# A hand-ordered SSD and feed-forward kernel: where two state additions stand, and a new order of steps

## The chip, the cores and the metric

One core of a Trainium2 chip runs the whole kernel in one launch. The metric is the device time of one execution in microseconds; the number given for a kernel is the median of its runs. Five engines take part, each with its own instruction queue that runs strictly in order: TensorE (PE, whose weight loads are shown apart as PEld), VectorE (DVE), ScalarE (ACT), GpSimd (POOL), and SyncE (SP), which only sends transfers here. Engines wait for each other through semaphores.

## What is computed

A state-space scan (Mamba-2 SSD) over 4 batches, 8 heads, 768 positions, head size 32 and state size 16, whose output, read as 3072 tokens of 256 features, goes through an RMS norm and a SwiGLU feed-forward of width 1536. The core of the reference:

```python
for c in range(nc):                       # chunks of 32 positions
    cum = np.cumsum(la, axis=-1)          # la = log of the decays a
    L = np.exp(cum[:, :, :, None] - cum[:, :, None, :]) * causal
    M = np.einsum('bhin,bhjn->bhij', Cc, Bc) * L
    y_intra = np.einsum('bhij,bhjd->bhid', M, xc)
    y_inter = np.einsum('bhin,bhnd->bhid', Cc, state) * np.exp(cum)[:, :, :, None]
    y[:, :, sl] = y_intra + y_inter
    Bx = np.einsum('bhjn,bhjd->bhjnd', Bc, xc) * np.exp(cum[:, :, -1:] - cum)[:, :, :, None, None]
    state = np.exp(np.sum(la, axis=-1))[:, :, None, None] * state + np.sum(Bx, axis=2)
...
rms = np.sqrt(np.mean(x * x, axis=-1, keepdims=True) + 1e-06)
xn = x / rms * rms_g
g = xn @ w_gate
silu = g * (1.0 / (1.0 + np.exp(-g)))
return (silu * (xn @ w_val) @ w_out).astype(np.float32)
```

## The kernel before

The 3072 tokens are worked on as twelve pairs of 256 tokens (for the scan) and six blocks of 512 (for the feed-forward). The kernel is a set of small functions, one for each kind of step, and one long text, `order` (from L1193), that lists 1548 steps by hand. A step reads `block:kind.arguments/slot`: `0:y.2/2` calls the kind `y` of block 0 for pair 2 and takes its PSUM buffers from pair slot 2. The steps are run through in this order, and each appends its instructions to the queues of the engines it uses. So the text alone sets in which order each engine does its work; there is no scheduler. A step that is moved in the text moves on every engine it uses, transfers included.

PSUM has three pair slots of two banks each, and two single banks that small results share (`bank`). Later, slots 0 and 1 are turned into the two buffers for gate and value products (step `switch`).

The kinds that matter here, with their lines:

- `fetch.k` sends a piece of a weight matrix (up to 512 KB) on SP's queue. The weights come as 64-bit floats and are converted on the chip: `pow.k` (ACT, L182, L183, L185), `man.k` (DVE, L192, L195), `wt.k` (DVE, L201). `x.p` and `bc.p` send the inputs x, and B and C, of a pair; `gcol` sends the norm's gains.
- The scan of a pair p: `mask`, `sums`, `exp` make the decays L (PE L426, L440, L447, ACT L455). `turn`, `T`, `Tt` transpose B and C (PE L505, L511). `scale` and `Td` put the decays on B and C. `g.p.q` (L555) and `gg.p` (L562) are the products C Bᵀ on PE. `L` and `L1` multiply them into the decays on DVE (L601, L607). `A.p` are the state additions, the sum of Bx, on PE (`additions`, L627); `S.p` makes the new states from them on DVE (L641 to L651). `y.p` are the outputs: for the first two pairs `first_outputs` (L668 for the state part, L677 for the part within a chunk), for later ones `outputs` (L699).
- Pairs 0 and 1 use chunks of 128 positions, later ones of 64. From pair 2 on, `outputs` writes the additions of the next pair into columns of its own y buffers. For pairs 1 and 2 the additions stand as steps of their own, `0:A.1` and `0:A.2`, which take single banks.
- After y: `sq` (ACT, L740 or L747) squares it, `yt` (DVE, L758, or ACT, L763) takes it with the gains, `r`, `row`, `rowe` and `parts` compute rows of decay sums for later pairs (PE L355, L1076; ACT L1089; DVE L362 to L369), `ms` (PE L773) and `rs` make the norm's factor, `xn` and `tx` the normed input and its differences.
- The feed-forward of block 0 begins as plain products: `early.f.s` on the inputs without norm (L837), `gate.f` (L827), with `norm`, `silu`, `hid` behind them. From there on, and in all later blocks, gate and value products use a form with seven products in place of eight: `P.k.j` (PE, L911), `take` (ACT copy, L917), totals `C` (DVE, L923), `silug`/`silu` (ACT, L932), `hidg`/`hid` (DVE, L936); `cw.j` makes the sums of weights it needs (DVE, L881). The output products go the same way: `O.k.f` (L1001), `Otake`, `Oadd`, and `out`, `quarter` send the results.
- `tok` (PE) and `tokout` (an ACT copy) make the sums of decays for all tokens, in a single bank.

The order of block 0 around the steps in question, before: `A.0 S.0 A.1 S.1 g.0.0 ... y.0 ... y.1 r.1 ... row.0 ... early.0.0 ... gate.2 ... gg.2 L1.2.2 L1.2.3 L.2.0 man.8 gate.3 ... A.2 S.2 ... gate.4 ... gate.5 ... y.2 S.3 ... P.2.3 P.1.3 take.1.3 turn.3 ...`

Of the kernel before, what the change touches and what calls it, by code (L numbers as in the profile page):

```python
# [20 lines left out]
def kernel(  # L21
# [35 lines left out]
    P = 128  # L57
    NB, NH, S, D = x.shape
# [5 lines left out]
    T = NB * S  # L64
# [108 lines left out]
    parts = {}  # L173
# [62 lines left out]
    mid = mids[:, 0]  # L236
# [382 lines left out]
    def additions(p, A_ps=None):  # L619
        s = st[p]  # L620
        if A_ps is None:
            A_ps = [bank("A_ps", (P, 2, 2, D)) for u in range(1 if p < 2 else 2)]
        ps["A", p] = A_ps = A_ps if p >= 2 else 2 * A_ps
        for i, u in chunks_of(p)[2]:
            r = slice(0, P) if p < 2 else halves[u]
            for q in range(NQ):
                nc.tensor.matmul(  # L627
                    out=A_ps[u][32 * q:32 * q + 32, i].rearrange("p t d -> p (t d)"),
                    lhsT=s["Bd"][r, i, 2 * q:2 * q + 2].rearrange("p t n -> p (t n)"),
                    rhs=s["x"][r, i, 2 * q:2 * q + 2].rearrange("p t d -> p (t d)"),  # L630
                    start=(i == 0), stop=True, tile_position=(r.start, 32 * q),
                    skip_group_check=True)
# [25 lines left out]
    def first_outputs(p, y):  # L658
# [27 lines left out]
        inter(1, False)  # L686
        del st[p], Ls[p]
# [260 lines left out]
    two = {}  # L948
# [216 lines left out]
    def of_chunk(n, fn):  # L1165
# [29 lines left out]
        0:never 0:after 0:mid 0:fetch.0 0:upto2 0:mids 0:ident16 0:idle.7 0:fetch.1 0:whole16  # L1195
        0:mask.0.0/0 0:whole 0:hmask 0:tmask 0:part 0:gcol 0:part2 0:sel 0:mask.1.1/2 0:after2 0:aT
        0:kinks 0:la0 0:mask.0.1/1 0:log4.0.4 0:fetch.5 0:r.0 0:eps 0:parts.0 0:log 0:d 0:log4.4.2
        0:dx 0:c*2 0:cx 0:scale.0 0:log4.6.2 0:turn.0.1 0:bc.2 0:T.0.1 0:Tt.0.0.1 0:sums.0.1
        0:Tt.0.1.1 0:exp.0.1 0:turn.0.0 0:Tt.0.1.0 0:T.0.0 0:sums.0.0 0:Tt.0.0.0 0:exp.0.0
        0:turn.1.1 0:T.1.1 0:scale.1 0:Tt.1.0.1 0:fetch.2 0:Tt.1.1.1 0:cc 0:g.0.1/1 0:L.0.1  # L1200
        0:turn.1.0 0:Tt.1.1.0 0:Tt.1.0.0 0:sums.1.1 0:T.1.0 0:exp.1.1 0:A.0 0:S.0 0:A.1 0:S.1
        0:g.0.0/0 0:man.0 0:pow.0 0:L.0.0 0:pow.1 0:wt.0 0:last.1 0:man.5 0:mask.1.0/1 0:middles
        0:Tl.1 0:sums.1.0 0:never16 0:fetch.4 0:exp.1.0 0:g.1.0/2 0:fetch.3 0:x.4 0:L.1.0 0:last.0
        0:Tl.0 0:scale.2 0:fetch.6 0:g.1.1/0 0:fetch.7 0:man.1 0:pow.5 0:L.1.1 0:y.0/1 0:wt.5 0:sq.0
        0:fetch.12 0:row.1 0:pow.3 0:rowout.1 0:yt.0 0:ydone.0 0:rowe.1 0:y.1/2 0:r.1 0:fetch.13
        0:row.0 0:man.2 0:fetch.9 0:wt.1 0:early.0.0/0 0:parts.1 0:man.6 0:mask.3/1 0:sums.3 0:pow.2
        0:wt.2 0:rowe.0 0:dT.2 0:sq.1 0:ms.0 0:yt.1 0:ydone.1 0:early.0.1 0:man.3 0:wt.3 0:mask.2/2
        0:sums.2 0:pow.6 0:fetch.8 0:wt.6 0:man.4 0:x.2 0:exp.3 0:early.1.0/1 0:rs.0 0:norm.0 0:xn.0
        0:pow.4 0:wt.4 0:fetch.10 0:man.7 0:dT.3 0:turn.2 0:early.1.1 0:norm.1 0:rowout.0 0:exp.2
        1:table 0:man.9 0:silu.0 0:hid.0 0:gate.2/0 0:T.2 0:Tt.2.0 0:Tt.2.1 0:Td.2 0:pow.7  # L1210
        0:fetch.14 0:wt.7 0:tx.0 0:gg.2/1 0:L1.2.2 0:L1.2.3 0:L.2.0 0:man.8 0:gate.3/2 0:pow.9
        0:fetch.11 0:silu.2 0:hid.2 0:pow.8 0:wt.9 0:wt.8 0:man.11 0:silu.3 0:hid.3 0:A.2 0:S.2
        0:x.3 0:pow.11 0:gate.4/1 0:silu.4 0:hid.4 0:cw.3 0:bc.3 0:scale.3 0:man.10 0:pow.12
        0:gate.5/0 0:silu.5 0:hid.5 0:pow.10 0:y.2/2 0:S.3 0:yt.2 0:sq.2 0:ydone.2 0:switch.1
        0:P.2.3 0:switch.0 0:P.1.3 0:take.1.3 0:turn.3 0:T.3 0:Tt.3.0 0:Tt.3.1 0:wt.10 0:wt.11
        0:P.1.4 0:P.6.3 0:take.6.3 0:man.12 0:Td.3 0:man.13 0:pow.14 0:gg.3/2 0:L1.3.3 0:L.3.0
        0:L1.3.2 0:bc.4 0:scale.4 0:P.2.4 0:P.7.3 0:bc.5 0:scale.5 0:x.5 0:y.3/2 0:wt.12 0:take.7.3
        0:C.11.3 0:P.5.3 0:silug.11.3 0:pow.13 1:S.0 0:fetch.18 0:P.4.3 1:dT.0 0:C.22.3 0:P.3.3
# [12 lines left out]
        0:sub.9 0:tx.1 1:P.6.1 1:take.1.0 1:Tt.0.0 0:hidg.22.5 0:o.11 1:Tt.1.0 2:bc.1 1:take.6.1
        1:P.7.1 0:cw.0 1:P.6.0 1:C.11.1 1:cw.2 1:P.5.1 1:take.7.1 1:C.22.1 1:P.4.1 1:P.2.0 1:C.11.0
        1:P.3.1 1:C.12.1 0:ex.10 0:ex.8 1:take.6.0 1:P.7.0 0:ex.9 1:bc.1 1:P.5.0 1:silu.22.1
        1:silu.21.1 1:bc.0 1:take.7.0 1:hid.21.1 1:P.1.2 1:hid.22.1 1:C.22.0 1:take.1.2 1:silu.11.0
        1:hid.11.0 1:P.4.0 1:silu.21.0 1:hid.21.0 1:silu.12.1 1:hid.12.1 1:P.2.2 1:C.11.2 1:scale2.1
        1:spread.0 1:two.4 1:silu.11.1 1:hid.11.1 1:Tt.0.1 0:table.1 1:P.6.2 1:take.6.2 1:P.3.0
        1:C.12.0 1:P.1.3 1:silu.11.2 1:hid.11.2 1:silu.22.0 1:hid.22.0 1:P.5.2 1:take.1.3 0:put.0
        0:put.3 1:P.7.2 1:take.7.2 1:C.22.2 0:put.2 1:P.6.3 1:take.6.3 1:P.2.3 1:C.11.3 1:silu.11.3
        1:two.2 1:silu.12.0 1:hid.12.0 1:P.4.2 1:silu.21.2 1:hid.21.2 1:P.7.3 1:take.7.3 1:silu.22.2
        1:hid.22.2 1:P.5.3 1:C.22.3 1:P.3.2 1:C.12.2 0:put.1 1:P.4.3 1:silu.21.3 1:hid.21.3  # L1240
        1:hid.11.3 1:silu.12.2 1:hid.12.2 1:x.0 1:P.1.4 1:take.1.4 1:P.3.3 1:C.12.3 1:Tt.1.1 1:Td.1
        2:dT.1 1:s.1 1:s3.1 1:P.1.5 1:take.1.5 1:Td.0 1:P.6.4 1:take.6.4 1:P.2.5 1:C.11.5 1:P.6.5
        1:take.6.5 1:scale2.0 1:P.2.4 1:C.11.4 1:silu.12.3 1:hid.12.3 1:g 1:L1.3 1:L1.2 1:L
        1:silu.11.4 1:hid.11.4 1:P.7.4 1:take.7.4 1:P.7.5 1:take.7.5 1:P.5.4 1:C.22.4 1:silu.22.3
        1:hid.22.3 2:dT.0 1:P.5.5 1:C.22.5 1:y.0 1:x.1 2:S.0 1:s.3 1:P.3.4 1:C.12.4 1:silu.11.5
        1:hid.11.5 1:P.4.5 1:silu.21.5 1:hid.21.5 1:s.0 1:P.4.4 1:silu.21.4 1:hid.21.4 1:silu.22.4
        1:hid.22.4 1:silu.22.5 1:hid.22.5 1:P.3.5 1:C.12.5 1:silu.12.5 1:hid.12.5 1:silu.12.4
        1:hid.12.4 1:O.2.0 1:O.2.1 1:s.2 1:y.1 2:S.1 1:sq 1:yt 1:s.5 1:O.2.2 1:O.1.0 1:O.1.1 1:O.4.0
        1:O.4.1 1:s.4 1:spread.2 1:sub.2 1:O.1.2 1:O.1.3 1:exps 1:O.1.4 1:O.1.5 1:s3.3 1:O.5.0
        1:O.5.1 1:s2.1 1:O.5.2 1:s2.2 1:s2.0 1:O.5.3 1:s2.3 1:s3.0 1:Otake.1 1:spread.1 1:sub.1  # L1250
        1:s3.2 1:ms 1:rs 1:O.5.4 1:O.5.5 1:s2.5 1:s2.4 1:rb 1:ex.2 2:turn.0 2:T.0 2:Tt.0.1 2:Tt.0.0
        1:O.6.0 1:s4.0 1:O.6.1 1:s4.1 1:O.6.2 1:s4.2 1:O.6.3 1:s4.3 2:turn.1 2:T.1 2:Tt.1.0 1:s3.4
        1:s3.5 1:O.6.4 1:s4.4 1:O.6.5 1:Otake.6 1:s4.5 1:O.4.2 1:O.4.3 1:O.7.0 1:O.7.1 1:O.7.2
        1:O.7.3 1:O.7.4 1:O.7.5 1:O.2.3 1:O.4.4 1:O.4.5 1:sub.0 1:ex.0 1:O.2.4 1:O.2.5 1:Otake.7
# [137 lines left out]
```

## Time and profile before

| | us |
|---|---|
| median of three runs | 403.85 (403.8 to 405.18) |
| the profiled execution | 404.06 |
| its span | 402.1 |
| PE busy in it | 394.8 |
| DVE busy | 297.9 |
| ACT busy | 224.5 |

The span is the time from the first to the last instruction; the rest of the execution's time lies around it. The granted TensorE clock is 0.999 of full. In views of groups, a line reads: line, engine, operation, output and input tiles, partitions by elements, count, then busy time and mean. In rows of the timeline the first two numbers are the start and the length in us, and a bracket at the end gives the idle time ahead of the row and what released it. Rows stand for several instructions in a run where they say x8 or the like; an fp32 matmul leaves two records. Ends of matmuls are modelled, so starts are the better measure on PE.

### The profile page before, as it was taken

What the parts mean: (1) busy time and instruction counts of PE and PEld (TensorE: products, weight loads), DVE (VectorE), ACT (ScalarE), POOL (GpSimd) and SP (SyncE); (2) the same over time, 40 slices, a digit from 0 to 9 for tenths busy, and PEclk for the clock granted to TensorE, in tenths of its full rate; (3) what the DMA queues carried; (4) which work ended last, traced back from release to release, by engine and by line L of the source; (5) the groups of instructions that cost most, each with busy time, mean ns of one, the idle gap of its engine ahead of it and who ended that gap; (6) DMA issues with size and microseconds to landing.
All of it is one profiled execution on the core that took longest, in us unless ns stands there. A gap on an engine that the chain in (4) does not pass through costs nothing.

```text
span 402.1 us, 9591 instructions
## 1 busy us (share of the span) xinstructions
PE 394.8 (98%) x3881; PEld 338.9 (84%) x3881; DVE 297.9 (74%) x686; ACT 224.5 (56%) x456; POOL 37.6 (9%) x57
## 2 busy tenths in 40 slices
PE   8989999999999999999999999999999999999997
PEld 5656477888888899888899988899988899988996
DVE  6999999999477997567689467887555767366871
ACT  3989887894684362753572653482645551445410
POOL 2210010001300021200102300021200010000000
PEclk9999999999999999999999999999999999999999
DMA  9989997129012306301223700202000001100001
GB/s 110 189 248 277 178 183 236 38 42 96 2 39 67 68 22 118 79 0 17 68 74 80 104 2 0 44 30 71 27 2 2 2 9 54 52 0 2 0 2 52
DMA packets 92595, 26.99 MB, mean 67 GB/s; under 512 B 77288, under 2 KB 86376, under 8 KB 92552
## 3 DMA queue, kind: packets, MB, share of 16 engines
q1 hardware_dynamic: 88392, 26.13, 30.1%
q10 hardware_dynamic: 4160, 0.26, 0.8%
q8 instruction: 30, 0.49, 0.5%
q14 instruction: 13, 0.11, 0.1%
HBM read 22.64 MB, written 3.74 MB: 66 GB/s over the span
## 4 chain that ended last, share of the span: by engine, by line
PE 91%; SPq 3%; DMA 2%; DVE 1%; ACT 1%; issue 0%
PE gate L911 28%; PE o L1001 24%; PE val L911 21%; PE o L943 5%; PE gate L827 4%; PE y L699 3%; PE gate L837 2%; PE g L562 2%; SPq L121 1%; DMA wr<-in_moe_w_val_dram 1%; PE tp L505 1%; SPq L128 1%; DMA br<-in_B_dram 1%; PE y L627 1%; SPq L160 1%; PE ms L777 0%
## 5 line engine op out<-in xcount | busy, mean ns | idle before, releaser
L923 DVE TENSOR_TENSOR c<-val,p 128x512 f32<-128x512 f32 x99 | 67.5, 688 | 33.8 <-PE val L911 29.6
L917 ACT COPY p<-gate 128x512 f32<-128x512 f32 x99 | 57.4, 581 | 53.2 <-PE gate L911 50.4
L911 PE MATMUL gate<-tx,sw 128*128 128x256 f32 x264 | 65.8, 381 | 0.0
L932 ACT ACTIVATE c<-c 128x256 f32<-128x256 f32 x99 | 39.5, 416 | 44.5 <-DVE c L923 44.5
L911 PEld LDWEIGHTS gate<-tx,sw 128*128 128x128 f32 x264 | 49.5, 190 | 7.1 <-issue 0.3
L936 DVE TENSOR_TENSOR h<-c 128x256 f32<-128x256 f32 x99 | 41.1, 426 | 18.2 <-ACT c L932 18.2
L911 PE MATMUL val<-xn,sw 128*128 128x256 f32 x132 | 33.6, 382 | 0.5 <-DVE c L923 0.5
L911 PE MATMUL val<-tx,sw 128*128 128x256 f32 x132 | 33.6, 383 | 0.1
L911 PE MATMUL val<-xn,wgv 128*128 128x256 f32 x132 | 33.7, 382 | 0.0
L911 PE MATMUL gate<-xn,wgv 128*128 128x256 f32 x132 | 33.4, 380 | 0.0
L911 PE MATMUL gate<-tx,wgv 128*128 128x256 f32 x132 | 33.0, 381 | 0.0
L475 POOL TENSOR_SCALAR_AFFINE_SELECT L<-L 64x512 f32<-64x512 f32 x32 | 23.7, 740 | 87.0 <-ACT L L473 85.8
L1001 PE MATMUL o<-wo,h 128*128 128x128 f32 x240 | 29.9, 276 | 0.0
L1001 PEld LDWEIGHTS o<-wo,h 128*128 128x128 f32 x240 | 28.5, 192 | 0.5 <-issue 0.2
L1001 PE MATMUL o<-two,h 128*128 128x128 f32 x240 | 28.9, 276 | 0.0
L1001 PE MATMUL o<-two,s 128*128 128x128 f32 x240 | 28.9, 276 | 0.0
L911 PEld LDWEIGHTS val<-xn,sw 128*128 128x128 f32 x132 | 24.8, 190 | 4.2 <-DVE c L923 0.9
L1001 PEld LDWEIGHTS o<-two,s 128*128 128x128 f32 x240 | 28.0, 192 | 0.4 <-issue 0.2
L911 PEld LDWEIGHTS val<-tx,sw 128*128 128x128 f32 x132 | 24.7, 190 | 3.9 <-DVE c L923 0.5
L1001 PEld LDWEIGHTS o<-two,h 128*128 128x128 f32 x240 | 27.8, 192 | 0.2 <-DVE s L967 0.2
L911 PEld LDWEIGHTS gate<-tx,wgv 128*128 128x128 f32 x132 | 24.8, 190 | 3.5 <-ACT c L932 0.2
L911 PEld LDWEIGHTS val<-xn,wgv 128*128 128x128 f32 x132 | 24.8, 190 | 3.5 <-issue 0.2
(188 smaller groups left out, 614.1 us busy)
## 6 DMA issues: line engine op xcount, KB each, us to landing
L<-rowd SPq DMA_DIRECT2D x32, 128.0 KB, 3.0
xr<-in_x_dram SPq DMA_DIRECT2D x24, 128.0 KB, 4.7
wr<-in_moe_w_out_dram SPq DMA_DIRECT2D x6, 512.0 KB, 7.0
wr<-in_moe_w_val_dram SPq DMA_DIRECT2D x5, 512.0 KB, 6.4
wr<-in_moe_w_gate_dram SPq DMA_DIRECT2D x5, 512.0 KB
out_dram<-ob SPq DMA_DIRECT2D x9, 256.0 KB, 2.2
br<-in_B_dram SPq DMA_DIRECT2D x22, 64.0 KB
cr<-in_C_dram SPq DMA_DIRECT2D x22, 64.0 KB, 2.4
```

The costliest lines, as they stand in the source:

```text
L475: nc.gpsimd.affine_select(out=L[r], in_=L[r], pattern=[[0, NH], [1, HC]], compare_op=ALU.is_ge, fill=0.0, base=0, channel_multiplier=-1)
L562: nc.tensor.matmul(out=g[u, P * i:P * i + P].rearrange("p (t m) -> p t m", t=2), lhsT=T[r, i, 0, u], rhs=T[r, i, 1:3, u], start=(first and ...
L699: nc.tensor.matmul(out=y[2 * k + u][rows, (2 * n + i) * HC:(2 * n + i + 1) * HC], start=(k, u, rows.start) not in opened, stop=True, skip_ ...
L827: nc.tensor.matmul(out=gv[:, k], lhsT=w[:, t, fs], rhs=xns[0][:, t], start=(t == 0), stop=(t == 1))
L837: nc.tensor.matmul(out=gv[:, k, tk], lhsT=w[:, t, fs], rhs=yts[0][:, t, tk], start=(s == 0 and t == 0), stop=(t == 1), skip_group_check=True)
L911: nc.tensor.matmul(out=dst[:, half[w]], lhsT=lhsT, rhs=rhs, start=(k in (1, 2, 5) and w == 0), stop=True, skip_group_check=True)
L917: nc.scalar.copy(out=t, in_=Xs[j])
L923: nc.vector.tensor_tensor(out=t, in0=Zs[j], in1=a, op=ALU.add)
L932: nc.scalar.activation(out=u, in_=src[:, half[0]], func=AF.Silu)
L936: nc.vector.tensor_tensor(out=hidden_tile(blk, j)[:, c // 10 - 1, c % 10 - 1], in0=u, in1=src[:, half[1]], op=ALU.mult)
L943: nc.tensor.matmul(out=o, lhsT=hs_[blk, f // 2][:, f % 2, k // 2, (k % 2) * P:(k % 2 + 1) * P], rhs=wo[:, f], start=opens, stop=(f == NF - ...
L1001: nc.tensor.matmul(out=o[t] if apart else o[:, t * P:(t + 1) * P], lhsT=lhsT[:, t], rhs=rhs, start=(k in (1, 2, 4, 5) and j == 0 and (apar ...
```

## The change

Two things change.

First, the additions of pairs 1 and 2. `first_outputs(p)` now ends with the additions of pair p + 1, written into columns 256 to 384 of the banks of y of pair p. So y.0 ends with the eight matmuls of A.1, and y.1 with the twelve of A.2; S.1 and S.2 read those columns. The steps `0:A.1` and `0:A.2` are gone from the order; `additions` takes a single bank of its own for pair 0 alone.

Second, the steps of the order are put in a new order from a place near the beginning (the 18th step is the first that differs) to the end. They are the same steps otherwise, 1546 in place of 1548. The number of instructions on PE, DVE, POOL and SP stays the same; ACT's program has 18 loads of function tables in place of 21. Line numbers behind L686 grow by two.

```diff
     def additions(p, A_ps=None):
         s = st[p]
         if A_ps is None:
-            A_ps = [bank("A_ps", (P, 2, 2, D)) for u in range(1 if p < 2 else 2)]
+            A_ps = [bank("A_ps", (P, 2, 2, D))]
         ps["A", p] = A_ps = A_ps if p >= 2 else 2 * A_ps
...
         intra(0, p == 0)
         intra(1, False)
         inter(1, False)
+        additions(p + 1, [y[:, u, 256:384].rearrange("p (i t d) -> p i t d", i=2, t=2)
+                          for u in range(p + 1)])
         del st[p], Ls[p]
...
-        0:turn.1.0 0:Tt.1.1.0 0:Tt.1.0.0 0:sums.1.1 0:T.1.0 0:exp.1.1 0:A.0 0:S.0 0:A.1 0:S.1
...
-        0:fetch.11 0:silu.2 0:hid.2 0:pow.8 0:wt.9 0:wt.8 0:man.11 0:silu.3 0:hid.3 0:A.2 0:S.2
...
+        0:T.1.0 0:Tt.1.0.0 0:Tt.1.1.0 0:fetch.2 0:man.0 0:g.0.1/0 0:L.0.1 0:bc.2 0:g.0.0/1 0:L.0.0
+        0:x.2 0:fetch.3 0:pow.0 0:wt.0 0:pow.1 0:last.1 0:Tl.1 0:man.1 0:fetch.9 0:g.1.1/2 0:L.1.1
+        0:g.1.0/0 0:gcol 0:middles 0:row.1 0:rowout.1 0:man.5 0:scale.2 0:pow.5 0:wt.5 0:fetch.6
+        0:mask.1.0/1 0:sums.1.0 0:exp.1.0 0:L.1.0 0:fetch.4 0:last.0 0:Tl.0 0:y.0/2 0:S.1 0:y.1/1
+        0:x.4 0:wt.1 0:fetch.8 0:fetch.7 0:fetch.11 0:man.2 0:r.1 0:pow.2 0:sq.0 0:yt.0 0:ydone.0
+        0:early.0.0/0 0:eps 0:pow.3 0:rowe.1 0:row.0 0:S.2 0:parts.1 0:wt.2 0:x.3 0:sq.1 0:yt.1
...
+        0:gate.2/0 0:silu.2 0:hid.2 0:tx.0 0:pow.9 0:wt.9 0:man.8 0:man.11 0:gate.3/1 0:silu.3
+        0:hid.3 0:pow.8 0:wt.8 0:Tt.2.1 0:Td.2 0:bc.3 0:scale.3 0:pow.11 0:cw.3 0:gate.4/2 0:silu.4
+        0:hid.4 0:fetch.10 0:man.10 0:gate.5/0 0:gg.2/1 0:L1.2.2 0:L1.2.3 0:L.2.0 0:y.2/2 0:pow.12
+        0:switch.1 0:P.2.3 0:silu.5 0:hid.5 0:switch.0 0:P.1.3 0:wt.11 0:pow.10 0:S.3 0:yt.2
+        0:fetch.18 0:sq.2 0:ydone.2 0:tok 0:tokout 0:wt.10 0:P.2.4 0:bc.5 0:scale.5 0:take.1.3
+        0:man.13 0:man.12 0:turn.3 0:T.3 0:Tt.3.1 0:Tt.3.0 0:Td.3 0:P.6.3 0:take.6.3 0:C.11.3 0:x.5
+        0:P.1.4 0:pow.14 0:wt.12 0:gg.3/2 0:L1.3.2 0:L.3.0 0:L1.3.3 0:P.7.3 0:take.7.3 0:bc.4
+        0:pow.13 0:P.5.3 0:scale.4 0:y.3/2 0:P.4.3 0:cw.4 2:bc.1 0:C.22.3 0:P.3.3 0:take.1.4 0:P.6.4
+        0:silug.21.3 1:S.0 0:silug.22.3 0:fetch.17 0:C.11.4 0:silug.11.4 0:take.6.4 0:P.5.4 0:P.7.4
...
+        5:s4.2 5:Otake.7 5:Oadd.22 5:Oadd.11 5:quarter.0.0 5:O.4.1 5:O.4.2 5:O.4.3 5:s4.5 5:Ot.3.0
+        5:Oadd.12.0 5:quarter.0.1.0 5:O.4.4 5:O.4.5 5:Oadd.21 5:out.1 5:Ot.3.1 5:Oadd.12.1
+        5:quarter.0.1.1
```

In the old order, `O.4.4 O.4.5 Oadd.21 out.1` of block 5 stand ahead of `Ot.3.0`.

## The prediction

> **What bounds the kernel now.** I read the page's engine shares first, then the busy time by stretches of the span, then TensorE's waits, then the chain that ended last, and last the rows around the places that the diff touches.
>
> ```profile
> PE 394.8 (98%) x3881; PEld 338.9 (84%) x3881; DVE 297.9 (74%) x686; ACT 224.5 (56%) x456; POOL 37.6 (9%) x57
> ...
> PE 91%; SPq 3%; DMA 2%; DVE 1%; ACT 1%; issue 0%
> ```
>
> The profiled execution took 404.06 us with a span of 402.1, so 1.96 us lie around the span; the median of the three runs is 403.85, 0.21 lower. TensorE is busy 98% of the span, and 91% of the chain of waits is TensorE's own work. The matmuls stay the same in number, shape and operands, so the change can only win what TensorE now loses. How much that is, the stretches tell (length, then busy us of PE, PEld, DVE, ACT, POOL with their counts, clock, DMA share, GB/s):
>
> ```profile
> 20.00:30.00 10.00, 8.32 (x113) 5.49 (x110) 9.72 (x24) 8.11 (x16) 1.74 (x2) 1.00 0.86 247
> 30.00:40.00 10.00, 10.00 (x88) 6.48 (x93) 9.55 (x18) 9.81 (x16) 0.00 (x0) 1.00 0.94 279
> 40.00:50.00 10.00, 10.00 (x77) 4.63 (x66) 9.79 (x24) 8.73 (x14) 0.00 (x0) 1.00 0.98 181
> 50.00:60.00 10.00, 9.77 (x190) 7.01 (x189) 9.39 (x22) 8.44 (x19) 1.03 (x1) 1.00 0.94 176
> 60.00:80.00 20.00, 19.48 (x231) 15.56 (x230) 19.17 (x48) 16.26 (x33) 0.74 (x1) 1.00 0.47 143
> 80.00:100.00 20.00, 20.00 (x97) 17.64 (x96) 18.91 (x40) 14.63 (x23) 1.73 (x2) 1.00 0.56 69
> ```
>
> From 30 us on PE misses 0.23 us in 50 to 60, 0.52 in 60 to 80, and nothing in 80 to 100. The holes it can lose sit ahead of 25.5 us and at three places behind. DVE, at 9.4 to 9.8 us of every 10 from 20 to 60, is the engine that a new order can easily push behind TensorE. The holes by name, and the stretch of the chain that runs into the first big product:
>
> ```profile
> PE r_ps L1076 <- ACT e_sb L1089: 0.9, 1, 0.9
> PE y L677 <- DVE L L601: 0.8, 1, 0.8
> PE val L911 <- DVE c L923: 0.5, 1, 0.5
> ...
> PE tp L505 <- ACT sq L747: 0.2, 1, 0.2
> ```
>
> ```profile
> 17.61 5.53 DMA wr<-in_moe_w_val_dram
> ...
> 24.78 0.17 ACT e_sb L1089
> 24.95 0.04 issue
> 25.00 0.71 PE r_ps L1076 x4
> 25.71 1.73 PE gate L837 x8
> ```
>
> A weight piece lands at 23.15 us, ScalarE converts it and only then copies e_sb (L1089), which row.0's matmuls (L1076) wait for, and early.0.0 (L837) stands behind them. From 25.5 us TensorE is nearly packed.
>
> **The change, part by part.**
>
> (1) Front, up to early.0.0. The new order puts row.0 behind early.0.0, so the wait of 0.9 us goes. What is late next is yt.0 on DVE (the operand of early.0.0). It starts at 22.98 now and lasts 0.86. In the new order DVE has wt.1 (0.34) and man.2 (0.65, the two rows from 23.77 to 24.42) ahead of it and loses never16 (0.4): 22.98 + 0.34 + 0.65 - 0.4 = 23.6, and up to 0.8 more if T.0.1, now ahead of scale.0, holds DVE until its transposes are there. gcol, which yt.0 multiplies with, is moved on SP's queue behind fetch.2, bc.2, x.2, fetch.3 and fetch.9; by adding their transfers at the rates of before it lands at 24.0 to 24.4. So yt.0 starts between 24.2 and 25.4 and early.0.0 0.85 later, at 25.0 to 26.2; I take 25.6 (gcol's bound with a little of the DVE delay). Behind it row.0 still costs its 0.5 of PE time, now with no wait since e_sb is long done. Before, early.0.0's time counts from 25.55; after, 25.6 + 0.5: **+0.5** (bounds -0.2 and +1.2).
>
> (2) The joined additions. A.1 (8 matmuls) and A.2 (12) no longer stand alone; they follow y.0 and y.1 in the same form of small tiles. The lone A.2 is this row:
>
> ```profile
> 44.14 0.43 PE L627 MATMUL A_ps<-xr,Bd 64*32 64x64 f32 x24
> 44.50 7.13 PE L827 MATMUL gate<-xn,wgv 128*128 128x512 f32 x16
> 51.56 0.69 PE L699 MATMUL y<-T,S 32*64 32x64 f32 x32
> 52.19 0.86 PE L699 MATMUL y<-L,xr 64*32 64x64 f32 x64
> 52.84 0.54 PE L627 MATMUL y<-xr,Bd 64*32 64x64 f32 x32
> ```
>
> From start to start the lone 24 records take 0.36, and the next product starts about 0.1 late, 0.46 in all; the joined 32 of pair 3 take 0.47, so 24 of them take 0.35, including the return to the full array, which y.1 pays anyway (about 0.1 to 0.2). So A.2 is worth **-0.2** (0 to -0.4). A.1 lies ahead of 25 us, where PE has room: nothing, its cover being the wait for yt.0; without cover it would cost some 0.2 (8 matmuls at the same rate, twice the rows).
>
> The cost: S.1 (DVE, L641) now reads a bank of y.0, which sq.0 (ACT) and yt.0 read too, and they take turns. In pair 3, where it is so already, y ends at 53.38, DVE's L641 takes 53.42 to 53.91, and ACT's next reading of that y begins at 54.35. So the price is up to 0.9 us for sq.0. It is hidden: sq.0 is behind pow.2 (2.2 us) on ACT, and ms.0, which needs it, stands behind early.0.0, row.0 and sums.3. If that cover went, ms.0 would stall 0.9.
>
> The Trainium skill (PSUM — Partial Sum Buffer, the section on bank collisions) speaks against this sharing: guard by bank and quadrant, since two engines in one at once is an error and not a short delay. The rule alone asks only that the two reads, 0.49 and about 0.6, do not overlap, so the sum by it would hold 0.5 where the row shows 0.9; in either case it lies behind pow.2.
>
> (3) y.2 directly behind gg.2. This is the new wait. Now gate.3 to gate.5 (11 us, 40.51 to 51.63) lie between g of pair 2 and y.2; in the new order gg.2, L1.2.2, L1.2.3, L.2.0 and y.2 are neighbours. y.2's third and fourth banks are those that g.2 leaves, so its first matmuls wait for the two L1 (DVE L607, 0.34 each) and its second half for L.2.0 (L601):
>
> ```profile
> 39.72 0.86 PE L562 MATMUL g<-T 32*64 32x128 f32 x32
> ...
> 41.85 0.75 DVE L607 TENSOR_TENSOR L<-g,L 128x256 f32<-128x256 f32 x2
> 42.52 0.68 DVE L601 TENSOR_TENSOR L<-g,L 128x512 f32<-128x512 f32 x1
> ```
>
> g's end to DVE's start about 0.2, then 0.34 + 0.34 + 0.68, and 0.2 back to TensorE: 1.75 from g's end to the products with L, of which y's other half (52.19 - 51.56 = 0.63) fills a part: **+1.05** of idle. Lower bound 0.5 (part of L1 done while g is still running); upper bound 2.1, if DVE comes to it as late as now (L.2.0 ends at 43.20, 2.6 behind g's end at 40.58). Against it, g and y now stand in one stretch of small tiles, one leaving and entering of that form less: **-0.3** (-0.2 to -0.4, from the starts around 39.7, 44.1 and 51.6). Behind the waiting matmuls stand switch and P.2.3, and all of TensorE; DVE waits about 1.7 us too, though it has been relieved by then of three gates' work.
>
> (4) Holes behind 50 us. turn.3's 0.4 (0.23 of it flagged) comes from following P.1.3 while sq.2 is not read out; tok and P.2.4 (over 2 us) now lie between. P.3.3 (0.62 between starts, 0.45 flagged) and P.5.4 (0.23) wait for DVE's totals; in the new order I find C.22.3 and C.11.4 in time, P.5.4 perhaps 0.15 late. -0.4 - 0.62 - 0.23 + 0.15 = **-1.1** (-1.25 to -0.4, the latter if the two P waits remain because DVE lost 1.7 us in (3)).
>
> (5) Blocks 1 to 5, 72 to 382 us: the same products. The least distance from a product to the one that needs its total is the same, but in two places (before 4:P.3.3 and 5:P.3.3) C.22 has only 0.03 to 0.1 us to spare. **+0.2** (0 to +0.5). The end: out.1's 256 KB now is sent about 0.7 us ahead of the last quarter, instead of 3 (before, it starts at 396.04 and the last two as one row from 398.14 to 399.83). The two transfers overlap: **+0.15** (0 to +0.3).
>
> (6) SP's queue. The new order of the fetches has bc.3, fetch.10 (held until pow.9, about 40.7), bc.4 and x.5 in the places that DVE meets next. With at most eight in flight and before's transfer times (0.65 of engine time for a bc, 1.34 for a 512 KB piece) I get bc.3 at 44 against scale.3 at 47, fetch.10 at 45.5 against man.10 at 49, bc.4 at 60 against scale.4 at 62: nothing, hidden by 2 to 3 us of DVE's other work. Should one be later than that, DVE, strictly in order, passes the lateness on to L1 and y.2 in full.
>
> **Sum:** 0.5 - 0.2 + 1.05 - 0.3 - 1.1 + 0.2 + 0.15 = +0.3. On the profiled 404.06 this gives 404.36; against the median, 404.15. I take **404.3 us**, span 402.4. What a measurement of this kernel can tell from no change is about 0.5%, 2.0 us: 401.83 to 405.87.
>
> **The rivals.**
>
> Slower, decided at y.2: DVE comes late to L1.2.2, because a fetch it needs (bc.3, fetch.10) is late, or because its queue is full (9.79 of 10 us in 40 to 50). For it: DVE has no slack there, and the order leaves nothing of TensorE's to cover it. Against it: gate.3 to gate.5 now run ahead of gg.2 and give DVE 11 us to catch up. It decides from a stall of 2.6 us on (1.05 in the sum + 1.5): with 3 us and the two P waits kept, 404.3 + 1.95 + 0.7 = 406.9. By the Trainium skill (TensorE: Matmul & The Clock Gate, Part 1) an idle window of about 3.4 us halves the clock; no wait in this profile is that long and the granted clock is 1.00 in all these stretches, so no row shows it; by the page a stall of that length would cost an estimated 1.7 us more. Chance 0.36.
>
> Faster: all lower bounds together, -0.2 - 0.4 + 0.5 - 0.4 - 1.25 = -1.75: 402.3, and a little more if early.0.0 starts at 24.6. For it: TensorE's holes named above are all moved. Against it: even this hardly passes the 2.0 us. Chance 0.12.
>
> The change does not do what it says: joining the additions is worth its -0.2 and the reordering shifts waits about without sum: 403.7. Chance 0.12.
>
> **How the numbers follow.** The forecast has the other 0.40. Its own range is 402.9 to 405.8 (the bounds of (1) and (3) on one side, those of (4) on the other). Out to the slower rival up to 407.2 and the faster one down to 402.2, about 2 in 10 are left out. Within 0.5%: nearly all of the forecast and of the last rival, 0.50; slower 0.37, faster 0.13.
>
> **What would show it.** Right: r_ps L1076 gone from TensorE's waits, a wait of y L699 for DVE's L of about 1 us near 52, no wait of tp L505 nor val L911 behind it, early.0.0 near 25.6. Wrong: a wait of several us at y L699 or g L562, a wait of DVE for a DMA between 40 and 60, or early.0.0 beyond 26.5; in the other direction a packed TensorE from 24.6 on. A wait behind 100 us would upset (5).

## The result

The changed kernel takes 405.04 us (median of 20 runs, 404.10 to 407.73); the kernel before, on the same chip, takes 403.81 (403.42 to 405.62). The ratio is 1.0028 with a 95% interval of 1.0015 to 1.0041: the change costs 1.2 us, less than the 0.5% that one measurement tells from no change, but with this many runs it is a loss and not zero. The forecast was 404.3 in a range of 402.2 to 407.2. Executions that the chip disturbed (477.3, 673.54, 1412.5 and 2277.7 us in the runs below) are left out of all comparisons, and the profiles of e3_fetch10_early and e7_waits_covered, which fell on two of them, are not read.

The profiled execution of the changed kernel took 404.52 us, its span 402.7 (before: 404.06 and 402.1). It loses 0.46 us against the profiled execution of before, which is less than half of what the medians differ by. So there are two things to explain: what is lost in every execution, and what is lost in some. Here are waits of TensorE in the changed kernel (engine, line, what is waited for, us in total, times, longest):

```profile
PE y L701 <- DVE L L607: 1.0, 1, 1.0
...
PE gate L913 <- DVE ob L1030: 0.4, 1, 0.4
...
PE e L440 <- DVE row L369: 0.4, 1, 0.4
PE gate L839 <- DVE yt L760: 0.3, 1, 0.3
```

The waits of before for e_sb (r_ps L1076), for the total c and for sq are gone, as the prediction said. The four shown have taken their place, and all four wait for DVE. Three more new ones (0.7 us at tp L511, 0.4 at y L668, 0.3 at g L555) lie between 12 and 21 us, ahead of early.0.0, which waits for yt.0 in any case. The first of the four is the predicted wait of y.2 behind gg.2. The chain of waits (start, length, what) shows what set its length:

```profile
46.28 4.63 DMA wr<-in_moe_w_gate_dram
50.91 0.02 issue
50.93 0.47 DVE m L192
51.40 0.02 issue
51.42 0.69 DVE m L195
52.11 0.35 DVE L L607
```

A weight piece (fetch.10) was sent at 46.28 and landed at 50.91. man.10 on DVE waited 0.45 us for it; L1.2.2, the next on DVE, came late by as much, and y.2 behind that. The prediction had this piece land at 45.5. The timeline of SP's queue shows why it did not:

```profile
39.72 0.41 SPq L160 DMA_DIRECT2D wr<-in_moe_w_out_dram  x1
40.23 0.41 SPq L160 DMA_DIRECT2D wr<-in_moe_w_gate_dram  x1
40.69 0.46 SPq L121 DMA_DIRECT2D br<-in_B_dram  x1
41.20 0.57 SPq L121 DMA_DIRECT2D cr<-in_C_dram  x1
41.82 3.73 SPq L121 DMA_DIRECT2D br<-in_B_dram  x1
45.59 0.59 SPq L121 DMA_DIRECT2D cr<-in_C_dram  x1
46.28 0.55 SPq L160 DMA_DIRECT2D wr<-in_moe_w_gate_dram  x1
```

The third transfer of bc.3 kept the queue for 3.73 us, where the two ahead of it took 0.46 and 0.57. Ahead stand two pieces of 512 KB each. The transfer that is held has no semaphore to wait for; sending it takes that long. (The chain names an ACT instruction, L185, ahead of the piece. It did not hold it: the queue's rows follow each other without a hole, and in the repetition the piece goes at 45.81, before ACT's L185 begins at 46.03.)

The same wait differs from execution to execution. In three profiles of kernels that are the same up to this place (the changed kernel, its repetition, and the kernel with later masks) y.2 waits 1.0, 0.5 and 1.5 us for L607. The first two are the same kernel. Here are man.10 and y.2 in the changed kernel, and then in its repetition:

```profile
50.93 0.45 DVE L192 TENSOR_SCALAR m<-wr 128x512 int32<-128x512 int32 x1 [0.45 <-DMA wr<-in_moe_w_gate_dram]
52.50 0.90 PE L701 MATMUL y<-T,S 32*64 32x64 f32 x28 [0.97 <-DVE L L607]
```

```profile
50.40 0.42 DVE L192 TENSOR_SCALAR m<-wr 128x512 int32<-128x512 int32 x1
52.00 0.89 PE L701 MATMUL y<-T,S 32*64 32x64 f32 x28 [0.46 <-DVE L L607]
```

In the repetition the piece is there in time, y.2 waits half as long, and the execution takes 404.08 us, which is level with the profiled 404.06 of before. The lowest runs of the two kernels still differ by 0.6 to 0.7 us (404.10 against 403.42, and 404.02 against 403.44 beside the repetition); these two profiles do not show why.

### The profile page after: what moved, and what is told of

It reads as the page before. It is cut to its first block, busy times and chain, and to the rows that moved or that the text cites. A ratio compares the mean times of both kernels' runs of the same rounds, so it can differ in the third digit from the quotient of the medians.

```text
span 402.7 us, 9564 instructions
## 1 busy us (share of the span) xinstructions
PE 393.9 (98%) x3881; PEld 338.3 (84%) x3881; DVE 296.7 (74%) x686; ACT 219.6 (55%) x453; POOL 36.0 (9%) x57
## 4 chain that ended last, share of the span: by engine, by line
PE 90%; DVE 4%; ACT 3%; DMA 1%; issue 0%; DVEq 0%
PE gate L913 29%; PE o L1003 22%; PE val L913 22%; PE o L945 5%; PE y L701 3%; PE gate L829 2%; PE g L562 1%; PE gate L839 1%; PE tp L505 1%; DMA wr<-in_moe_w_gate_dram 1%; ACT L L455 1%; PE y L627 1%; PE e L426 1%; DVE tx L890 1%; ACT e L183 1%; ACT e L182 1%
## 5 line engine op out<-in xcount | busy, mean ns | idle before, releaser
L475 POOL TENSOR_SCALAR_AFFINE_SELECT L<-L 64x512 f32<-64x512 f32 x32 | 22.5, 703 | 97.3 <-ACT L L473 95.7
L1019 ACT COPY v<-o 128x256 f32<-128x256 f32 x15 | 5.6, 371 | 41.9 <-PE o L1003 41.9
L913 PEld LDWEIGHTS gate<-xn,wgv 128*128 128x128 f32 x132 | 24.5, 190 | 4.2 <-DVE ob L1030 0.8
```

The costliest lines, as they stand in the source:

```text
L475: nc.gpsimd.affine_select(out=L[r], in_=L[r], pattern=[[0, NH], [1, HC]], compare_op=ALU.is_ge, fill=0.0, base=0, channel_multiplier=-1)
L913: nc.tensor.matmul(out=dst[:, half[w]], lhsT=lhsT, rhs=rhs, start=(k in (1, 2, 5) and w == 0), stop=True, skip_group_check=True)
L1019: nc.scalar.copy(out=ts[k], in_=halves_of(Os["X"]))
```

## The experiments

The theories. A, the late pieces: fetch.10 and bc.3 come just in time or too late for DVE, differently in each execution; y.2 stands directly behind gg.2, so TensorE has no cover, and after a long wait its clock falls as well. B, the neighbours: y.2 behind gg.2 costs the same in every execution. C: the costs lie elsewhere, in sums.3 (0.4 us) and at 221 us (0.59).

**a0_same.** No edit.

> The changed kernel once more, unchanged, as the base for the others on this chip. Expected 405.0 us (median over 20 runs so far 405.04, single runs from 404.1 to 407.7) and about 1.2 us above the kernel before. If its runs spread again over 2 us or more while those of before stay within 0.5 us, something that varies from run to run holds TensorE up; a wait that is the same in each run (y.2 behind gg.2, the 0.59 us at 221 us) would give the same time in all.

Measured: 405.22 us (404.02 to 408.36), 403.83 before; ratio 1.0039 (1.0018 to 1.0060). The time comes again, and the spread too (4.3 us). The 34 runs of before beside it spread over 2.0 us, more than the 0.5 that I had expected: 27 lie at 403.44 to 404.15 and 7 at 405.03 to 405.39. Of the 32 runs of the changed kernel so far 13 have a mean granted clock of 0.987 to 0.996; none of the 34 runs of before beside it has one below 0.999.

**e1_man10_later.**

```diff
-        0:fetch.10 0:man.10 0:gate.5/0 0:gg.2/1 0:L1.2.2 0:L1.2.3 0:L.2.0 0:y.2/2
+        0:fetch.10 0:gate.5/0 0:gg.2/1 0:L1.2.2 0:L1.2.3 0:L.2.0 0:y.2/2 0:man.10
```

> man.10 (DVE, waits for the landing of fetch.10) stands behind y.2 instead of ahead of gate.5 and gg.2, so no DMA stands between gg.2 and y.2 any more. Theory A (the late piece): in the profile man.10 holds DVE 0.45 us and so L1.2.2; without it y.2's wait falls from 1.18 us to about 0.7, and since the landing varies, the median falls by more, 0.8 to 1.2 us (to 404.0), and the spread becomes narrower. Theory B (the neighbours): y.2 directly behind gg.2 costs 1.05 us whatever the piece does; the median falls by at most 0.45 us (404.6) and the spread stays. Theory C (the costs lie elsewhere: sums.3's 0.4 us and the 0.59 us at 221 us): no change, 405.0.

Measured: 406.6 us (404.51 to 407.36), ratio 1.0052 (1.0035 to 1.0068): slower, where both theories said faster. The wait of y.2 is 0.5 us in the profile, and only one of 11 runs has a low clock. But man.10 (1.2 us of DVE) now stands ahead of S.3, yt.2 and sq.2 come later, and TensorE meets a wait of 0.8 us at tok for sq.2 (L749). The wait moved on by three steps. That fits the two lowest runs, 404.51 and 404.57, some 0.4 us above the lowest of the changed kernel. The median lies higher because six of the eleven runs stand at 406.6 or more; the profiled one of these began 1.5 us late (last section), and why there are so many is open. So the time says nothing of A. The 0.5 us, here and in the repetition, speaks against B's 1.05 whatever the piece does.

**e2_gate5_between.**

```diff
-        0:gate.5/0 0:gg.2/1 0:L1.2.2 0:L1.2.3 0:L.2.0 0:y.2/2
+        0:gg.2/1 0:L1.2.2 0:L1.2.3 0:L.2.0 0:gate.5/0 0:y.2/2
```

> gate.5 (3.5 us of TensorE's work) stands between L.2.0 and y.2 instead of ahead of gg.2. Theory B (the neighbours): y.2's wait of 1.18 us goes, one more leaving and entering of the small tiles costs 0.3 us: 404.1 to 404.2. Theory A (the late piece): the same gain, since 3.5 us hide a late man.10 as well, and the spread becomes narrower; in single runs in which the piece lands over 3 us late a part remains. Theory C (costs elsewhere): 405.0 or, with the added leaving and entering, 405.3.

Measured: 404.76 us (403.65 to 405.97), ratio 1.0020 (1.0006 to 1.0035), 0.46 below the changed kernel in the same comparison, with intervals that overlap. The waits of y.2 are gone from the profile, its highest run is 2.4 us lower, and one run of 12 has a low clock. The wait that is gone is what A and B both expect. The time lies between their 404.1 to 404.2 and C's 405.0 to 405.3 and decides nothing.

**e4_masks_later.**

```diff
-        2:ex.2 2:ex.3 3:Tt.0.1 2:O.2.3 2:O.2.4 2:O.2.5 2:Otake.7 2:Oadd.22 3:P.1.0 3:take.1.0 2:Oadd.21 3:P.1.1 3:take.1.1
+        3:Tt.0.1 2:O.2.3 2:O.2.4 2:O.2.5 2:Otake.7 2:Oadd.22 3:P.1.0 3:take.1.0 2:Oadd.21 3:P.1.1 3:take.1.1 2:ex.2 2:ex.3
```

> ex.2 and ex.3 of block 2 (ACT's exponentials L473 and POOL's four masks L475, 217.29 to 220.87 us) stand behind P.1.1 of block 3 instead of ahead of tx. Theory C1: DVE's four differences for tx take 0.42 us each alone but 0.75 to 0.87 us while POOL works; without POOL beside them they take 0.45 and end 1.0 us earlier, Oadd.21 with them, and the 0.59 us that P.1.1 waits at 221 us goes: 404.45. If DVE is not slowed by POOL, the four differences keep their 2.8 us and nothing changes: 405.0.

Measured: 404.70 us, ratio 1.0014 (0.9995 to 1.0033), 0.52 below the changed kernel beside it, again with intervals that overlap. DVE's rows of the changed kernel, with POOL's masks from 217.29 to 220.87 beside them:

```profile
217.57 0.42 DVE L890 TENSOR_TENSOR tx<-xn 128x256 f32<-128x256 f32 x1
218.03 0.75 DVE L890 TENSOR_TENSOR tx<-xn,tx 128x256 f32<-128x256 f32 x1
218.70 0.87 DVE L890 TENSOR_TENSOR tx<-xn 128x256 f32<-128x256 f32 x1
219.49 0.86 DVE L890 TENSOR_TENSOR tx<-xn,tx 128x256 f32<-128x256 f32 x1
```

and of this kernel, where POOL does nothing there:

```profile
217.96 0.42 DVE L890 TENSOR_TENSOR tx<-xn 128x256 f32<-128x256 f32 x1
218.41 0.43 DVE L890 TENSOR_TENSOR tx<-xn,tx 128x256 f32<-128x256 f32 x1
218.76 0.42 DVE L890 TENSOR_TENSOR tx<-xn 128x256 f32<-128x256 f32 x1
219.09 0.42 DVE L890 TENSOR_TENSOR tx<-xn,tx 128x256 f32<-128x256 f32 x1
```

The same instructions take 2.9 us with POOL beside them (three of the four about twice as long) and 1.7 alone, and P.1.1's wait for Oadd.21 (L1030) is gone from the profile. This cost of 0.59 us is shown by the trace, not by the times; it belongs to C. This profile also has y.2's longest wait of the three, 1.5 us. There DVE waited twice for transfers, 0.66 us for bc.3's B and 0.52 us for fetch.10. So both pieces can be late.

**e3_fetch10_early.**

```diff
-        0:bc.3 0:scale.3 0:pow.11 0:cw.3 0:gate.4/2 0:silu.4 0:hid.4 0:fetch.10 0:man.10
+        0:fetch.10 0:bc.3 0:scale.3 0:pow.11 0:cw.3 0:gate.4/2 0:silu.4 0:hid.4 0:man.10
```

> fetch.10 is sent ahead of bc.3 instead of behind it (the one change to the changed kernel), so that the queue's limit no longer holds it until 46.28 us; it should land at about 45 us instead of 50.91, and man.10 find it there. Theory A (the late piece): y.2's wait is 0.67 us (the price of the neighbours alone, as in the profiles with a punctual piece) in every run; no run shows a clock below 0.999, whereas 13 of the 32 runs of the changed kernel showed 0.987 to 0.996; the median falls from 405.1 to about 404.3 and what remains are two groups 1.5 us apart, which come from the start of the kernel. Rival theory (the piece is not the cause of the low clocks): the low clocks stay in 3 to 5 of 12 runs, median 405.0.

Measured: 405.79 us, ratio 1.0050 (1.0030 to 1.0069), with six runs: not the gain to 404.3 that A expected. The next-but-one kernel holds the same edit and shows why.

**e4_fetch10_later.**

```diff
-        0:fetch.10 0:man.10 ... 0:S.3 0:yt.2 0:fetch.18
+        0:fetch.18 0:fetch.10 0:man.10 ... 0:S.3 0:yt.2
```

> The suspected cost made larger: fetch.18 (512 KB) is sent ahead of fetch.10, so that the piece man.10 waits for lands some 2 us later still. Theory A: y.2's wait grows by about 2 us (to about 3 us), most runs show a clock of 0.987 to 0.996, and the median rises by 2 to 4 us (407 to 409). Rival theory: DVE or TensorE have something else to wait for and the time stays at 405.1.

Measured: 405.72 us, ratio 1.0040 (1.0023 to 1.0057), five runs, and no low clock. The dose did not arrive: in the profile the piece is sent at 47.31, only 1.0 us later than in the changed kernel, and this execution's start was 1.5 us late (last section), so that DVE came to the piece later too and waits only 0.17 us for it. It decides nothing.

**e5_three_mended.** The edits of e2_gate5_between, e3_fetch10_early and e4_masks_later together.

> The changed kernel with the three places mended together: fetch.10 ahead of bc.3, gate.5 between L.2.0 and y.2, and the masks ex.2 and ex.3 behind P.1.1. If the three costs are separate, its fast group falls from 404.1 to 404.1 - 0.67 + 0.3 - 0.59 = 403.1 us, the median to 403.2 to 403.8 (by how many runs fall into the group 1.5 us above), no low clocks, so 0.1 to 0.6 us below the kernel before. If they are not separate (one hides another): 404 or more.

Measured: 405.01 us (403.78 to 407.72), ratio 1.0029 (1.0009 to 1.0048), and four low clocks in 12 runs. Of the three, two are covered by the runs above; the one that fails is the early fetch.10. DVE's rows:

```profile
50.11 0.43 DVE L488 TENSOR_TENSOR Bd<-br,d_sb 128x256 f32<-128x256 f32 x1 [2.33 <-DMA br<-in_B_dram]
```

With fetch.10 ahead of it, bc.3 is sent later, and scale.3, which stands on DVE ahead of man.10, waits 2.33 us for it. y.2's wait grew to 1.1 us for L607, with 0.5 more for hid.4 (L862), in spite of gate.5. In this full queue one piece came earlier only at another's cost.

**e6_only_joined.** The order of the kernel before with the first part of the change.

```diff
-        0:A.0 0:S.0 0:A.1 0:S.1 0:g.0.0/0
+        0:A.0 0:S.0 0:g.0.0/0
...
-        0:y.0/1 0:wt.5
+        0:y.0/1 0:S.1 0:wt.5
...
-        0:yt.1 0:ydone.1 0:early.0.1
+        0:yt.1 0:ydone.1 0:S.2 0:early.0.1
...
-        0:hid.3 0:A.2 0:S.2 0:x.3
+        0:hid.3 0:x.3
```

(x.2 and x.4 have also changed places.)

> The first part of the change alone: the order of the kernel before, but y.0 and y.1 end with the additions of the next pair, S.1 and S.2 stand behind y.0 and yt.1, and the loads of x for pairs 2 and 4 have changed places. My step (2): -0.2 us from the lone A.2 of 0.46 that becomes 0.26, and A.1 at nothing: 403.6. Rival: y.1 has to wait for S.1, which now stands behind y.0, and the front is late by 0.5 to 0.8 us: 404.3. Low clocks and the wider spread should be absent either way.

Measured: 405.68 us (404.38 to 408.26), ratio 1.0049 (1.0027 to 1.0071): 1.8 us slower than before, where step (2) said 0.2 faster. The chain of waits runs through DVE here from 22 us on, and S.2 is a part of it (two more S L651 follow these rows):

```profile
31.35 0.33 DVE A L641 x2
31.68 0.20 DVE S L651
```

Joined to y.1, A.2 must be read out before y.1's banks are used again. So S.2, 1.2 to 1.3 us of DVE, moves from 47.65, where it stood in the kernel before, to 31 us (this execution began 1.5 us late, see the last section), where DVE is what the next gates wait for. It is not shown to be the whole of the 1.8 us: x.2 and x.4 differ too, and S.1 stands later. By the starts on TensorE, the profile's 3.2 us of longer span are 1.5 at the start, 0.7 from there to y.2, and 1.0 in y.3, where TensorE stands still without a wait that the profile shows:

```profile
65.01 0.25 PE L701 MATMUL y<-L,xr 64*32 64x64 f32 x3 [0.76 <-issue]
```

Of the waits between the start and y.2, one of 0.44 us is for yt.1, which stands ahead of S.2 on DVE; two of 0.26 and 0.30 us stand behind it. So S.2 can account for a part only.

**e7_waits_covered** and **e8_and_sums3_later.** e7:

```diff
-        0:bc.3 0:scale.3 0:pow.11 0:cw.3 0:gate.4/2 0:silu.4 0:hid.4 0:fetch.10 0:man.10 0:gate.5/0 0:gg.2/1 0:L1.2.2 0:L1.2.3 0:L.2.0 0:y.2/2
+        0:bc.3 0:pow.11 0:cw.3 0:gate.4/2 0:silu.4 0:hid.4 0:fetch.10 0:gg.2/1 0:L1.2.2 0:L1.2.3 0:L.2.0 0:scale.3 0:man.10 0:gate.5/0 0:y.2/2
```

and the edit of e4_masks_later. e8 adds:

```diff
-        0:mask.3/2 0:sums.3 0:exp.3 0:ms.0 0:rs.0
+        0:ms.0 0:mask.3/2 0:sums.3 0:exp.3 0:rs.0
```

> The changed kernel with gate.5 between L.2.0 and y.2, with the two DVE steps that wait for late pieces there (scale.3 for bc.3, man.10 for fetch.10) behind L.2.0 so that gate.5 covers them, and with the masks ex.2 and ex.3 behind P.1.1. Theory A (the two late pieces, through DVE, make y.2's wait long and variable): y.2 does not wait any more even where a piece is 2 us late; fast group 404.1 - 0.67 + 0.3 - 0.59 = 403.1, a second group 1.5 us above (slow start of TensorE's clock), no clocks below 0.999; median 403.2 to 404.0. Rival (the spread comes from elsewhere): spread and low clocks as in the changed kernel, median 404.4 or more.

> The same, and mask.3, sums.3 and exp.3 behind ms.0, so that TensorE does not wait for parts.1 (0.40 us at 28.57 in the changed kernel). If that wait is a cost of its own: 0.4 us less than the kernel beside it. If what is hidden behind it (ms.0 waits for sq.1) takes its place: the same time, the wait now at ms L775.

Measured: e7 404.94 us, ratio 1.0008 (0.9989 to 1.0026); e8 403.64 us (403.09 to 405.17), ratio 0.9992 (0.9976 to 1.0009), and no run of e8 has a clock below 0.999. So e8 gives back what the change cost: it is level with the kernel before, not measurably better. TensorE's rows in e8 around the two places:

```profile
27.52 1.10 PE L775 MATMUL ms<-sq,mean 128*128 128x512 f32 x2
...
48.09 3.70 PE L829 MATMUL gate<-xn,wgv 128*128 128x512 f32 x8
51.72 0.69 PE L701 MATMUL y<-T,S 32*64 32x64 f32 x32
```

ms.0 goes ahead at 27.52 without a wait, and y.2 runs without a hole behind gate.5. From the start of early.0.0 to that of early.0.1 TensorE takes 4.55 us (25.02 to 29.57), where it takes 4.82 in the changed kernel (25.31 to 30.13), so 0.27 of the 0.4 us of sums.3's wait come back. The times do not show it as a cost of its own: the four lowest runs of e7 (403.01 to 403.62) lie no higher than those of e8 (403.09 to 403.53), and both fit the 403.1 that e7's expectation named. e7's median is above its expectation because seven of its 11 runs lie above 404.5, three of them with low clocks (two of 0.987), though its order covers y.2 as e8's does; why is open.

**e9_piece_5us_late.**

```diff
-        0:fetch.10 0:man.10 ... 0:P.2.4 0:bc.5 0:scale.5
+        0:bc.5 0:fetch.10 0:man.10 ... 0:P.2.4 0:scale.5
```

> The suspected cost made much larger: the four transfers of bc.5 stand ahead of fetch.10 in SP's queue, so that it is sent at about 50 us instead of 46.28 and lands about 55. Theory A: y.2's wait becomes 4 to 6 us, the median rises by 3 to 6 us, and nearly all runs have a granted clock of 0.987 to 0.996, which the windows behind 52 us show (the clock falls after the wait, for some us). Rival (the low clocks have another cause): the time rises by the wait alone and the clock stays at 1.0.

Measured: 408.01 us (407.24 to 410.82), ratio 1.0103 (1.0074 to 1.0132); five of six runs have a clock of 0.992 or 0.996. DVE, then TensorE, then the stretches of 2 us (length, busy us of PE, PEld, DVE, ACT, POOL with counts, granted clock, DMA share, GB/s):

```profile
52.14 0.43 DVE L192 TENSOR_SCALAR m<-wr 128x512 int32<-128x512 int32 x1 [2.20 <-DMA wr<-in_moe_w_gate_dram]
```

```profile
50.70 0.30 PE L701 MATMUL y<-T,S 32*64 32x64 f32 x4
53.69 0.89 PE L701 MATMUL y<-T,S 32*64 32x64 f32 x28 [2.69 <-DVE L L607]
...
56.06 2.07 PE L913 MATMUL val<-xn,wgv 128*128 128x256 f32 x4
```

```profile
52.00:54.00 2.00, 0.31 (x8) 0.21 (x8) 1.82 (x5) 1.79 (x3) 0.00 (x0) 1.00 0.37 144
54.00:56.00 2.00, 1.97 (x120) 1.71 (x116) 1.75 (x3) 0.41 (x1) 0.00 (x0) 0.77 0.04 8
56.00:58.00 2.00, 2.00 (x12) 1.58 (x6) 1.71 (x7) 1.24 (x6) 0.00 (x0) 0.50 0.58 92
58.00:60.00 2.00, 2.00 (x10) 1.78 (x9) 1.97 (x4) 0.51 (x3) 0.74 (x1) 0.88 1.17 126
```

The piece was 2.2 us late (less than the edit was meant for), y.2 waited 2.69 us, and some 1.4 us after the wait was over TensorE went on at half its clock until 58.5 us: the four matmuls of P.2.3 take 2.07 us where they take 1.13 otherwise. So a late piece is paid for twice. The half clock, from about 55.1 to 58.5, is 1.7 us of lost time (0.23, 0.50 and 0.12 of three stretches of 2 us). The sum nearly comes out: this execution is 2.72 us longer than the profiled one of the changed kernel, although its first r_ps starts 0.53 earlier (5.57 against 6.10), so 3.25 in all, against 1.72 more of waiting and the 1.7.

**e10_tok_later.**

```diff
-        0:tok 0:tokout 0:wt.10 0:P.2.4 0:bc.5
+        0:wt.10 0:P.2.4 0:tok 0:tokout 0:bc.5
```

(in the order of e8)

> The kernel of e8_and_sums3_later with tok and tokout behind P.2.4 (2 us of TensorE's work more ahead of tok, which waits there for sq.2, 0.41 us from start to start at 55.70). If the wait goes: 0.3 to 0.4 us less than that kernel in the fast group (402.7 to 403.2), and median 403.3 if about a third of the runs fall into the group 1.5 us above. If turn.3, which is then the first behind y.2 to wait for sq.2, takes it over: the same time.

Measured: 404.49 us, ratio 1.0014 (0.9995 to 1.0032); its lowest run is 1.04 above that of e8. tok was itself the cover of two others:

```profile
56.41 1.13 PE L913 MATMUL val<-xn,wgv 128*128 128x256 f32 x4 [0.63 <-DVE wgv L201]
...
58.76 1.13 PE L913 MATMUL gate<-tx,sw 128*128 128x256 f32 x4 [0.46 <-ACT p L919]
```

P.2.4 now comes before wt.10 is ready, and P.6.3 waits for take.1.3, which stands behind tokout on ACT. Neither of the two outcomes that I had named came.

## Why the prediction was right, and where it was not

The direction, the place and the range were right; the size was too small: the sum said +0.3, the profiled executions differ by +0.46 (their spans by 0.6) and the medians by +1.2. The starts of ms.0 and of P.2.3 on TensorE, before and then after, divide the span into three stages:

```profile
28.39 1.13 PE L773 MATMUL ms<-sq,mean 128*128 128x512 f32 x2
53.31 1.13 PE L911 MATMUL val<-xn,wgv 128*128 128x256 f32 x4
```

```profile
29.16 1.12 PE L775 MATMUL ms<-sq,mean 128*128 128x512 f32 x2
54.55 1.13 PE L913 MATMUL val<-xn,wgv 128*128 128x256 f32 x4
```

Up to ms.0 the change costs 0.77 (forecast +0.5), from there to P.2.3 0.47 (forecast -0.2 + 1.05 - 0.3 = +0.55), and behind it it wins 0.64 (forecast -1.1 + 0.2 + 0.15 = -0.75). That the sum came near the profile is in part luck: the errors have both signs, and the middle stage came out only with a late piece that step (6) had put at nothing. In the repetition, whose piece was in time, the middle stage is -0.04 (29.17 to 54.05) and the span 402.2, 0.1 above that of before. Point by point:

(1) Front. early.0.0 starts at 25.31, waiting for yt.0 as forecast (24.79 for yt.0; bounds 24.2 to 25.4). It starts when the first of yt.0's two instructions ends, 0.52 behind yt.0 and not 0.85. What held yt.0 was man.2, which it follows on DVE without a gap, and not gcol, by which the sum went; man.2's first instruction took 0.82 us (at 23.58) with POOL working beside it from 23.40 to 24.25, and 0.28 in the kernel before. Missing was a step: sums.3, behind row.0, waits 0.4 us for parts.1.

(2) The joined additions. The lone A.2 is gone on TensorE, worth about its 0.46 and more than the 0.2 of the sum, since the joined one stands at 23.93, where TensorE has 0.32 us to wait for yt.0 in any case. What failed is that the step priced only the matmuls and the shared bank. It left out that S.2 moves along on DVE. In the changed kernel it stands right ahead of parts.1:

```profile
25.79 0.21 DVE L641 TENSOR_TENSOR A<-y,tmask 128x64 f32<-128x64 f32 x1
25.92 0.91 DVE L651 SCALAR_TENSOR_TENSOR S<-S,fcol,A 128x64 f32<-128x64 f32 x3
26.74 0.42 DVE L362 CAST first<-r_ps 128x256 bf16<-128x256 f32 x1
```

Its 1.25 us (25.58 to 26.83, with one more L641 ahead of these rows) are what makes parts.1, and so sums.3, late. The price of sq.0 for the shared bank was hidden, as said: TensorE has no wait for sq.0.

(3) y.2 behind gg.2. The mechanism was right, the middle value (1.05) was not: with the piece in time y.2 waits 0.46 us, the lower bound of 0.5, and the 0.97 of the changed kernel's profile holds about as much again from the late piece. (The working's own numbers, 1.75 - 0.63, give 1.12.) The spread, 0.5 to 1.5 us in three profiles, was the part that the rival held, not the forecast.

(4) All three waits (turn.3, P.3.3, P.5.4) are gone: -1.25, the lower bound, against -1.1.

(5) Named the wrong places. 4:P.3.3 and 5:P.3.3 have no wait; P.1.1 of block 3 has 0.59 us, because POOL's masks run beside DVE's four differences and nearly double three of them. I had taken DVE's durations as fixed. The end costs nothing visible: from the start of the last DVE instruction to the end of the last sending it is 0.67 us in both kernels (399.16 to 399.83, and 399.75 to 400.42), and the span ends 2.3 us behind that in both.

(6) SP's queue, the step that failed. It said fetch.10 would land at 45.5 and the rest be hidden by 2 to 3 us. It landed at 50.91, 5.4 us later; the largest part of that is the sending of one bc.3 transfer, which took 3.73 us, some 3.2 more than usual. Without these 3.2 the piece would have been there before DVE came to it (an estimate from the rows: 47.7, against 50.48). I had counted the sending at its usual half a microsecond and limited only the number in flight, though the profile of before had such rows too (3.13 us at 19.54, 3.00 at 42.03). With that, the slower rival's mechanism is what happens: a piece that DVE needs is late, and y.2 has no cover. The prediction had named a wait of DVE for a transfer between 40 and 60 us as a sign of being wrong, and it is there, 0.45 us. The rival had its decisive point at a stall of 2.6 us, and e9 reached 2.69; the three profiles of this order stay at 0.5 to 1.5.

The range of the forecast itself, 402.9 to 405.8, does not quite follow from the bounds that it names: those of (1) and (3) add up to 406.05.

What the runs leave open: no profile of the changed kernel itself fell on an execution with a low clock, so that its 13 low clocks come from y.2's wait is an inference from e9 (which has the wait and the half clock in one profile), from e8 (which has neither), and from the counts: where gate.5 covers y.2 (e2, e7, e8, e10), 5 of 47 runs have a clock below 0.999, against 13 of 32. These five suggest that there is at least one more cause. Two things do not fit a simple price either. The half clock of e9 is a mean clock of 0.996 and 1.7 us; but five of the changed kernel's runs at 0.996 took only 404.88 to 405.08 us, at most 1.1 above its lowest, and a clock of 0.987 (some 5 us of lost clock) came with 406.13 to 406.43. So a part of the low clock seems to have fallen where it cost nothing. How the 1.2 us of the medians divide into late pieces, low clocks and late starts is not shown.

## What to carry to other kernels

When work is joined to a step to save a change of tile form on one engine, look at what must now be read out early on another: here 0.46 us of TensorE were paid with 1.25 us of a fuller DVE. Two dependent steps made neighbours cost their latency even when every piece is on time, and they make every late transfer visible; e8 gave the loss back with 3.5 us of independent work between them, and with the steps that wait for transfers moved behind the first of the two (among other edits). And a queue's sending times must be read from the rows of a full queue, not of an empty one.

## What the runs showed of the hardware

- After a wait of 2.69 us TensorE's granted clock went to 0.50 for about 3.4 us, some 1.4 us after work had resumed (e9, one profile). The Trainium skill (TensorE: Matmul & The Clock Gate, Part 1) says that the clock halves after an idle window of about 3.4 us; here a shorter wait was enough, and the measured wait decides; the loss, 1.7 us, is the one that the prediction had estimated from the page.
- TensorE's matmuls come to their full rate at the start either at about 5 us or at about 10, with the same instructions, while the granted clock of the profile reads 1.00 in both. r_ps (L355), at 6.10 in both rows below, takes 0.67 us in the changed kernel and 1.19 in e2_gate5_between. Everything behind it is 1.5 to 1.7 us later in the second, and so in the profiles of e1, e4_fetch10_later and e6; SP's queue is not later by as much, and a piece has that much more time. Runs 1.4 us above the lowest group occur in the kernel before too (7 of 34 in one comparison, 8 of 16 in another); that these have the same cause is not shown.
- DVE's fp32 differences of two operands (128x256, L890) took 0.42 us alone and, but for the first of the four, 0.75 to 0.87 us beside POOL's masks (L475).
- Sending one transfer of 64 KB in 64-byte packets held SP's queue for 3.73 us behind 1 MB of weights.

```profile
6.10 0.67 PE L355 MATMUL r_ps<-mids,la 128*128 128x256 f32 x2 [0.23 <-issue]
```

```profile
6.10 1.19 PE L355 MATMUL r_ps<-mids,la 128*128 128x256 f32 x2
```
